# Attention and soft mixture of experts on one core: the attention loop written by pairs of heads, both heads' products with v in one run of 64-column tiles and one bank, and transposed x copied out of its bank by VectorE

## The chip, the core and the metric

The kernel runs on one core of one Trainium2 chip. Its engines work side by side, each through its own list of instructions in order: TensorE (PE, whose weight loads the profile shows apart as PEld), VectorE (DVE), ScalarE (ACT), GpSimd (POOL) and SyncE (SP), which here issues nearly all transfers from and to the main memory. An engine that waits for another holds everything that stands behind the waiting instruction in its list. The metric is device time in microseconds of one execution; a kernel is run several times and the median counts.

## The reference

Eight batches of twelve heads attend causally over 448 positions with 64 columns a head; the result is laid out as a matrix x of 3584 rows by 768 columns. A soft mixture of eight experts with four slots each follows.

```
scores = 0.125 * q @ k.T, -1e9 above the diagonal
attn = softmax(scores);  x = attn @ v               # per head; heads side by side in x
logits = x @ phi                                    # 3584 x 32
d = softmax of logits over the 3584 rows;  slot_input = d.T @ x
slot_out[e] = relu(slot_input[e] @ w1[e]) @ w2[e]   # 768 -> 1024 -> 768, four slots an expert
out = softmax of logits over the 32 slots @ slot_out
```

All is float32. The weights w1 and w2 are 50 MB together, q, k and v about 33 MB.

## The kernel before, in words

**Two stages.** The first goes through the 96 heads, as 48 pairs that share 128 partitions, and fills x, the logits and the slot inputs. The second goes through the experts and then through the rows of the output. Weight tiles of 768 KB (128 x 1536, `load_w`) are fetched in both: 23 (numbers 0 to 22) during the first stage, one with every other pair; numbers 23 to 34 into memory that the first stage gives back at its end (pool `wt1`), and the rest into tiles that are used again. SP issues its transfers in order, so a weight tile whose memory is still in use holds back those after it.

**One head.** The scores lie transposed, keys on partitions, in one tile of two banks (`s`; three such tiles, six of the eight banks). `scores1` adds the causal mask (a product of `tri` with a bf16 identity) and the product of k with q; `max_keys` (DVE, three instructions: one that transposes and reduces, two short ones) takes the maxima; `max_row` brings them into a row by a transpose on PE into `rt` and a reduction on DVE into `mr`; `max_spread` (POOL) writes them into rows of `r2`; `scores2` adds to the scores the product of `k2` with `r2`, which holds the row maxima and the rounding rest of q; `exps` (ACT) writes the exponentials to `pt`; `attv` multiplies them with v, with a column of ones for the sum, in tiles of 128 rows by 64 columns of the array; `norm` (DVE) divides by the sum and writes x. Around it, for each pair, ACT rounds k and q (`cast_k`, `cast_q`) and copies k (`copy_k2`), and POOL computes the rests (`sub_k`, `sub_q`). Each raw k or q (448 KB) has one of three buffers and is fetched anew as soon as its rest is computed.

**Where the order comes from.** Every engine runs in the order in which the program is written. Table `ORDER` gives it for a head: head i has its `scores2` and `exps`, head i+1 its `max_row`, head i+2 its `scores1`, and head i-1 its products with v and its `norm`, so PE alternates between scores and products of different heads.

**Two small banks.** Of the eight banks, one (`po`) takes the products with v of one head, four blocks of 65 columns, and one (`misc`, tag "m") is shared by everything small, one user at a time: `rt`, the transposed x of a pair (`xt`, copied to memory by ACT as `xts`), the logits of a batch in three parts (`g`, from two pairs each, `next_logits`), the slot input (`sp`, twice a batch, `dispatch`) and two transposes once a batch (`tp`, `logits_e`). In the table the steps with `g`, `xt`, `sp` and `tp` stand between `scores2` and `attv`.

**The last block of queries** has 64 rows, not 128. Its four products take the first 64 columns of the array and leave the other 64 empty; the products of the other three blocks come in twos, one for each half of the array.

Of the kernel before, what the change touches and what calls it, by code (L numbers as in the profile page):

```python
# [17 lines left out]
P = 128  # L18
# [14 lines left out]
NR, XB, XT = 2, 3, 3  # L33
# [14 lines left out]
ORDER = (  # L48
# [4 lines left out]
)  # L53

SC0, SC1, SC2, SC3 = 576, 0, 320, 512
RW, RC, RF = 96, 4, 20
CQ0 = (0, 128, 256, 384)
# [29 lines left out]
def attention_soft_moe(ctx: ExitStack, tc: tile.TileContext, qk, va, phi, w1, w2, out):  # L87
# [17 lines left out]
    qd_, kf_ = [fix.tile([P, 2, S], F32R, name="qd0")], [fix.tile([P, 2 * S + KP], F32R, name="ks0")]  # L105
    x_[1] = fix.tile([P, NCH, 3 * P], F32, name="x1")
    qd_.append(fix.tile([P, 2, S], F32R, name="qd1"))
    zero = fix.tile([P, P // 2], F32, name="zero")
    r_ = [fix.tile([P, RW], F32, name=f"r{i}") for i in range(2)]
    kf_.append(fix.tile([P, 2 * S + KP], F32R, name="ks1"))  # L110
# [3 lines left out]
    kf_.append(fix.tile([P, 2 * S + KP], F32R, name="k2"))  # L114
    *ks_, k2_ = (k[:, 0:2 * S].rearrange("p (h s)->p h s", h=2) for k in kf_)
# [88 lines left out]
    nc.vector.memset(zero, 0.0)  # L204
    nc.vector.tensor_copy(out=identb, in_=ident)
    for i in range(NR):
        nc.gpsimd.memset(r2_[i][0:64, :, :].bitcast(F32), 0.0)
        if i == 0:
            nc.vector.memset(k2_[0:64, :, :].bitcast(F32), 1.0)
    nc.vector.memset(pob, 0.0)  # L210
    for k in kf_:
        nc.vector.memset(k[:, 2 * S:2 * S + KP].bitcast(F32), 0.0)
    for i in range(2):
        nc.vector.memset(r_[i], -3.0e38)
# [12 lines left out]

    def cast_q(p, hs=slice(0, 2)):
        if p < NPAIR:
            nc.scalar.activation(out=qd_[p % NR][:, hs], in_=st["raw", 0, p][:, hs], func=AF.Copy)  # L230

    def cast_k(p, hs=slice(0, 2)):
        if p < NPAIR:
            nc.scalar.activation(out=ks_[p % NR][:, hs], in_=st["raw", 1, p][:, hs], func=AF.Copy)

    def sub_k(p, hs=slice(0, 2), eng=None):
        if p < NPAIR:
            ks = ks_[p % NR][64:P, hs]
            (eng or nc.gpsimd).tensor_tensor(out=ks, in0=st["raw", 1, p][64:P, hs], in1=ks, op=ALU.subtract)

    def copy_k2(p, hs=slice(0, 2)):
        if p < NPAIR:
            nc.scalar.activation(out=k2_[64:P, hs], in_=ks_[p % NR][0:64, hs],
# [8 lines left out]
    def scores1(i, part):  # L252
# [3 lines left out]
        ks, qd = kf_[p % NR], qd_[p % NR]  # L256
# [69 lines left out]
    def scores2(i, cs):  # L326
# [4 lines left out]
        k2, r2 = kf_[NR], r2_[p % NR]  # L331
# [9 lines left out]
    def attv(i, qcs):  # L341
        if not 0 <= i < NHD:
            return
        p, h = divmod(i, 2)
        pt, v, po = pt_[i % 2], va_[p % 2], st.get(("po", i), po0)
        begun = st.setdefault(("begun", i, id(po)), set())
        for qc in qcs:
            for c in range(qc + 1):
                col = SCOL[c] + P * (qc - c)
                for u in range(0, P if qc < 3 or i == NHD - 1 and c == 3 else 64, AW):  # L350
                    nc.tensor.matmul(po[u:u + AW, qc], pt[:, col + u:col + u + AW], v[:, c, h],
                                     start=u not in begun, stop=c == qc, skip_group_check=True)
                    begun.add(u)

    def norm(i, k):
        if not 0 <= i < NHD:
            return
        p, h = divmod(i, 2)
        if k == 0:
            if i % 6 == 0:  # L360
                xn = x_[p // 3 % XB]
                st["xn", p // 3] = xn
                for k in range(3):
                    st["x", p + k] = xn[:, :, P * k:P * k + P]
            sm = st["sm", i] = moe.tile([P, NCH], F32, tag="sm", name=f"sm{i}", bufs=2)
            nc.vector.tensor_scalar(out=sm, in0=st.get(("po", i), po0)[:, :, HD], scalar1=EPS, scalar2=None, op0=ALU.add)
        elif k == 1:
            nc.vector.reciprocal(out=st["sm", i], in_=st["sm", i])
        else:
            sm = st.pop(("sm", i))  # L370
            nc.vector.tensor_tensor(out=st["x", p][:, :, HD * h:HD * h + HD], in0=st.get(("po", i), po0)[:, :, 0:HD],
                                    in1=sm.unsqueeze(2).to_broadcast([P, NCH, HD]), op=ALU.mult)

    def xtrans(p):
# [5 lines left out]
        nc.scalar.activation(out=xt, in_=pt, func=AF.Copy)  # L383
# [64 lines left out]
    plan, plan_a = {}, {}  # L448
    for b in range(NB):
        o, last = 12 * b, b == NB - 1  # L450
        for j in range(PPB if not last else PPB - 2):
            plan_a[o + 2 * j + 4] = lambda p=b * PPB + j: xtrans(p)
        for j, r in ((0, 9), (2, 11)):
            plan[o + r] = lambda b=b, j=j: next_logits(b, j, misc(f"g{b}_{j}"))
        if not last:
            plan[o + 15] = lambda b=b: (next_logits(b, 4, misc(f"g{b}_4")), logits_b(b, lt))
            plan_a[o + 17] = lambda b=b: logits_e(b)
# [440 lines left out]
```

## Time and profile before

| | |
|---|---|
| median of 3 runs | 432.06 us (430.77 to 432.63) |
| profiled execution | 430.89 us |
| its span, first to last instruction | 429.2 us |
| busy: PE, PEld | 396.0, 317.6 us |
| busy: DVE, ACT, POOL | 297.6, 287.5, 266.2 us |
| mean clock granted to PE | 0.979 of full |
| read from and written to memory | 107.25 and 11.01 MB |

The span falls in two. Up to about 331 us the heads run, at about 240 GB/s of transfers; from there to the end the experts and the output run, at about 410 GB/s. A line of the profile names the engine, the operation and out<-in by the program's names; numbers of buffers are left out, so `r` stands for `r_` and for `r2_`, `ks` for both buffers of k. All instructions are recorded under line 71, that of the helper that keeps the order, so tiles tell them apart. An instruction's duration and the next one's start overlap by some 0.07 us on DVE, so steps are read from start to start.

### The profile page before, as it was taken

What the parts mean: (1) busy time and instruction counts of PE and PEld (TensorE: products, weight loads), DVE (VectorE), ACT (ScalarE), POOL (GpSimd) and SP (SyncE); (2) the same over time, 40 slices, a digit from 0 to 9 for tenths busy, and PEclk for the clock granted to TensorE, in tenths of its full rate; (3) what the DMA queues carried; (4) which work ended last, traced back from release to release, by engine and by line L of the source; (5) the groups of instructions that cost most, each with busy time, mean ns of one, the idle gap of its engine ahead of it and who ended that gap; (6) DMA issues with size and microseconds to landing.
All of it is one profiled execution on the core that took longest, in us unless ns stands there. A gap on an engine that the chain in (4) does not pass through costs nothing. (4 is left out here: it accounts for less than half of the span.)

```text
span 429.2 us, 14091 instructions
## 1 busy us (share of the span) xinstructions
PE 396.0 (92%) x5782; PEld 317.6 (74%) x5782; DVE 297.6 (69%) x861; ACT 287.5 (67%) x400; POOL 266.2 (62%) x216
## 2 busy tenths in 40 slices
PE   6898999999999999999999999999989998998740
PEld 3687888898898889888988888898868654544430
DVE  4687788778777877787787877778775477423440
ACT  5587879787887888887878788878865211333330
POOL 5799998888888788887887888888861000000000
PEclk8999999999999999999999999999999999999985
DMA  7476777777677776777776776677759999999997
GB/s 266 137 246 225 216 267 258 248 250 224 222 260 256 238 237 213 246 254 243 237 229 226 256 269 236 211 227 268 268 210 344 411 413 422 425 419 411 400 393 328
DMA packets 34481, 119.18 MB, mean 278 GB/s; under 512 B 3824, under 2 KB 8944, under 8 KB 32880
## 3 DMA queue, kind: packets, MB, share of 16 engines
q1 hardware_dynamic: 34272, 118.01, 77.5%
q8 instruction: 46, 0.75, 0.7%
q10 hardware_dynamic: 144, 0.27, 0.2%
q14 instruction: 19, 0.16, 0.1%
HBM read 107.25 MB, written 11.01 MB: 276 GB/s over the span
## 5 line engine op out<-in xcount | busy, mean ns | idle before, releaser
L71 ACT ACTIVATE pt<-s 128x1024 f32<-128x1024 f32 x96 | 98.2, 1023 | 57.2 <-PE s L71 51.8
L71 PEld LDWEIGHTS po<-va,pt 128*64 128x64 f32 x3040 | 117.8, 137 | 22.1 <-issue 21.6
L71 PE MATMUL po<-va,pt 128*64 128x65 f32 x3040 | 131.0, 225 | 0.0
L71 DVE TRANSPOSE_TENSOR_REDUCE r<-s 128x32 f32<-128x1024 f32 x96 | 118.2, 1231 | 2.4 <-PE s L71 2.0
L71 POOL TENSOR_TENSOR r<-qk,qd 64x896 fp32r<-64x896 f32 (+1 forms) x50 | 101.2, 2023 | 6.5 <-ACT qd L71 2.7
L71 POOL TENSOR_TENSOR ks<-qk,ks 64x896 fp32r<-64x896 f32 (+1 forms) x47 | 97.8, 2080 | 6.6 <-ACT ks L71 3.5
L71 POOL TENSOR_SCALAR_AFFINE_SELECT r<-mr 14x448 fp32r<-14x448 f32 x96 | 61.9, 645 | 47.5 <-DVE mr L71 43.4
L71 PE MATMUL s<-qd,ks 128*128 128x448 f32 (+3 forms) x384 | 76.5, 310 | 2.3 <-DVE ks L71 2.3
L71 PE MATMUL s<-r,k 128*128 128x320 f32 (+3 forms) x384 | 65.0, 290 | 3.5 <-ACT k L71 2.1
L71 PEld LDWEIGHTS s<-r,k 128*128 128x128 f32 (+1 forms) x384 | 54.3, 176 | 8.3 <-POOL r L71 5.6
L71 PEld LDWEIGHTS s<-qd,ks 128*128 128x128 f32 (+1 forms) x384 | 55.3, 182 | 3.1 <-DVE ks L71 2.5
L71 DVE TENSOR_SCALAR sm<-po 128x4 f32<-128x4 f32 x95 | 15.4, 162 | 52.9 <-PE po L71 51.8
L71 ACT ACTIVATE ks<-qk 128x896 fp32r<-128x896 f32 (+1 forms) x50 | 46.1, 923 | 8.1 <-DMA qk<-in_qk_dram 4.3
L71 ACT ACTIVATE qd<-qk 128x896 fp32r<-128x896 f32 (+1 forms) x50 | 46.1, 923 | 1.8 <-DMA qk<-in_qk_dram 1.7
L71 ACT ACTIVATE k<-ks 64x896 fp32r<-64x896 f32 (+1 forms) x49 | 45.8, 934 | 1.1
L71 DVE TENSOR_TENSOR x<-po,sm 128x256 f32<-128x256 f32 x95 | 40.3, 425 | 3.3
L71 PE MATMUL s<-tri,identb 128*128 128x64 bf16 (+2 forms) x288 | 39.6, 234 | 0.0
L71 PEld LDWEIGHTS <-identb 128*128 128x128 bf16 x339 | 35.0, 107 | 4.9 <-issue 3.1
L71 DVE TENSOR_REDUCE r<-r 128x16 f32<-128x32 f32 x192 | 34.1, 177 | 5.4
L71 PE MATMUL rt<-ident,r 128*76 128x128 f32 x96 | 28.8, 300 | 2.7 <-DVE sm L71 0.8
L71 PE MATMUL xt<-ident,x 128*128 128x128 f32 x188 | 29.7, 281 | 0.1
L71 DVE TENSOR_REDUCE mr<-rt 14x32 f32<-14x128 f32 x96 | 25.8, 269 | 3.8 <-PE rt L71 3.6
(136 smaller groups left out, 360.6 us busy)
## 6 DMA issues: line engine op xcount, KB each, us to landing
qk<-in_qk_dram SPq DMA_DIRECT2D x94, 448.0 KB, 4.0
w<-in_w_dram SPq DMA_DIRECT2D x43, 768.0 KB, 6.9
w<-in_w_dram SPq DMA_DIRECT2D x10, 1536.0 KB, 19.1
va<-in_va_dram SPq DMA_DIRECT2D x47, 260.0 KB, 3.2
out_dram<-ot SPq DMA_DIRECT2D x16, 384.0 KB, 6.7
out_dram<-ot SPq DMA_DIRECT2D x2, 1536.0 KB, 9.3
qk<-in_qk_dram SPq DMA_DIRECT2D x4, 224.0 KB, 3.4
hw<-in_w_dram SPq DMA_DIRECT2D x1, 768.0 KB, 6.4
```

What stands on the lines that cost most here:

```text
L71: return self._tc.keep_in_program_order(op(*args, **kwargs))
```

## The change

- The loop goes by pairs. `block(p)` writes for both heads a = 2p and a+1, in this order on PE: `scores2(a)`, `scores1(a+2)`, `scores2(a+1)`, [`tp`], `xt` of the pair before, `scores1(a+3)`, `attv(a)`, `rt(a+2)`, `attv(a+1)`, the last blocks of both heads (`attv3`), `rt(a+3)`, then `sp` or `g` where the pair has one.
- Both heads' products have one bank: seven blocks of 65 columns. The last blocks of the two heads are one block, head a in the upper 64 partitions and head a+1 in the lower; `attv3` alternates between them, so each fills one half of the array. `rt` takes 64 columns rather than 76, the same shape of tile as the products.
- `norm` is done once a pair: one sum, one reciprocal, one product for the full blocks of both heads and one for each last block.
- The copy of `xt` to memory goes from ACT to DVE, behind `max_keys(a+2)` and ahead of `max_keys(a+3)`.
- `sub_q(p+1)` stands in block p, no longer in pair p-1; the fetch of the raw k of pair p+3, which takes the buffer that it frees, follows it in the block, and so does that raw k's `cast_k(p+3)`, as the last of ACT's work. The fetch of v and of a weight tile stands at the block's start.
- `sp` of the seventh batch's second half is issued in the last block, behind `attv(a)`; before it was issued in the pair 45.
- Before the loop, `scores1` of head 2 and two runs of filling products go away and the work on the maxima of head 1 comes in. Two tiles rather than three hold `xts`; the rows 64 to 127 of the last block in x are zeroed once.

On PE, around the logits of pairs 14 and 15 (`rt34` to `rt37` are the rows of maxima of heads 34 to 37). Before:

```order
L71 MATMUL po_130<-va0_94,pt1_99 64x65 x16
L71 MATMUL rt36_2100<-ident_120,r0_90 76x128 [waits DVE_49,Activation_49]
...
L71 MATMUL s35_1994<-r21_96,k2_95 66x64
L71 MATMUL g2_2_2121<-xts14_1958,phi0_226 32x128 [waits DVE_49]
...
L71 MATMUL po_130<-va1_98,pt0_97 64x65 [waits DMAHW4_49]
L71 MATMUL po_130<-va1_98,pt0_97 64x65 x15
L71 MATMUL rt37_2154<-ident_120,r1_91 76x128 [waits DVE_49,PE_49]
```

Now:

```order
L65 MATMUL rt34_1982<-ident_119,r0_89 64x128 [waits DVE_49]
L65 MATMUL po_129<-va0_93,pt1_98 64x65 [waits Activation_49]
L65 MATMUL po_129<-va0_93,pt1_98 64x65 x11
...
L65 MATMUL rt35_2011<-ident_119,r1_90 64x128 [waits DVE_49,PE_49]
L65 MATMUL g16_2020<-xts14_1846,phi0_223 32x128 [waits DVE_49]
L65 MATMUL g16_2020<-xts14_1846,phi0_223 32x128 x3
L65 MATMUL g16_2020<-xts15_1949,phi1_224 32x128 x4
L65 MATMUL s34_1929<-r21_95,k2_94 128x448 [waits Activation_49,Pool_49]
```

Before, a whole head's products (16 instructions of the program) stood between the `g` and the next `rt`, and `scores2` ahead of `g`. Now `g` follows `rt35` at once, and `scores2` of head 34 follows `g`.

On DVE, in the block of pair 16 (heads 32 and 33). Now:

```order
L65 TENSOR_REDUCE r0_89<-s34_1929 128x2x16 [waits PE_49]
L65 TENSOR_REDUCE r0_89<-r0_89 128x2x8 [waits DVE_49]
L65 TENSOR_REDUCE r0_89<-r0_89 128x6 [waits DVE_49]
L65 COPY xts15_1949<-xt15_1944 128x512 [waits PE_49]
L65 TENSOR_REDUCE r1_90<-s35_1952 128x2x16 [waits PE_49]
L65 TENSOR_REDUCE mr34_1996<-rt34_1982 14x32 [waits PE_49,Pool_49]
L65 TENSOR_REDUCE r1_90<-r1_90 128x2x8 [waits DVE_49]
L65 TENSOR_REDUCE r1_90<-r1_90 128x6 [waits DVE_49]
L65 TENSOR_SCALAR sm16_2009<-po_129 128x7 [waits PE_49]
L65 TENSOR_REDUCE mr35_2013<-rt35_2011 14x32 [waits PE_49,Pool_49]
```

Before, `rt34` and `rt35` were reduced a head apart, each ahead of the maxima of the next head's scores; now the maxima of both heads, with the copy of `xt` between them, stand in a row ahead of `mr35`.

On SP, the weight tiles of `wt1` from number 25 on. Before:

```order
L71 DMA w_5532<-in_w_dram 128x1536 [waits Activation_49]
L71 DMA w_5534<-in_w_dram 128x1536 [waits DMAHW6_49,DVE_49,PE_49]
L71 DMA w_5536<-in_w_dram 128x1536 [waits PE_49,Activation_49]
```

Now:

```order
L65 DMA w_5417<-in_w_dram 128x1536 [waits DMAHW7_49,DMAHW6_49,Pool_49]
L65 DMA w_5419<-in_w_dram 128x1536 [waits DMAHW5_49,PE_49]
L65 DMA w_5421<-in_w_dram 128x1536 [waits DVE_49,PE_49]
L65 DMA w_5423<-in_w_dram 128x1536 [waits DVE_49]
```

The second row of the first piece and the third of the second are weight tile 26. By the addresses in both programs it takes the place of one buffer of k and of the end of `x1`, and PE's part of its wait is for the `sp` of the seventh batch's second half, which reads `x1` last. Tile 24 (first row now) waits for `sub_q` of the last pair in both.

```diff
-NR, XB, XT = 2, 3, 3
+NR, XB, XT = 2, 3, 2
...
-    pob = ps_1.tile([P, NCH * VC], F32, name="po")
-    po0 = pob.rearrange("p (a b)->p a b", b=VC)
+    pob = ps_1.tile([P, NQ * VC], F32, name="po")
+    po2 = pob.rearrange("p (a b)->p a b", b=VC)
+    po0 = po2[:, 0:NCH]
...
-            nc.tensor.transpose(out=st["rt", i][0:RW - RF, 0:P], in_=r_[i % 2][:, RF:RW], identity=ident)
+            nc.tensor.transpose(out=st["rt", i][0:AW, 0:P], in_=r_[i % 2][:, RF:RF + AW], identity=ident)
...
+    def attv3(p):
+        for c in range(NCH):
+            for h in range(2):
+                col = SCOL[c] + P * (NCH - 1 - c)
+                nc.tensor.matmul(po2[AW * h:AW * h + AW, NQ - 1], pt_[h][:, col:col + AW], va_[p % 2][:, c, h],
+                                 start=False, stop=c == NCH - 1, skip_group_check=True)
...
         xt = st["xt", p] = xtp.tile([P, 512], F32, tag="xt", name=f"xts{p}", bufs=XT)
-        nc.scalar.activation(out=xt, in_=pt, func=AF.Copy)
+        nc.vector.tensor_copy(out=xt, in_=pt)
...
+    def block(p):
+        a, b = 2 * p, p // 6 - 1
+        last, m6 = p == NPAIR - 1, p % 6
...
+        if p % 2 and p // 2 < RES:
+            load_w(p // 2)
+        scores2(a, range(NCH))
+        exps(a)
+        scores1_all(a + 2)
+        for k in range(3):
+            max_keys(a + 2, k)
+        scores2(a + 1, range(NCH))
+        if m6 == 2 and b >= 0 and p > 6:
+            logits_e(b)
+        if p:
+            xtrans(p - 1)
+        exps(a + 1)
+        scores1_all(a + 3)
+        max_keys(a + 3, 0)
+        sub_q(p + 1)
+        load_qk(p + 3, 1)
+        sub_k(p + 2)
+        load_qk(p + 3, 0)
+        if m6 == 1 and p > 6:
+            logits_d(b, lt)
+        copy_k2(p + 1)
+        cast_q(p + 2)
+        cast_k(p + 3)
+        if last:
+            attv(a, [(qc, qc, FULL if qc < 3 else FULL[0:1]) for qc in range(NCH)], po0, begun)
+            dispatch(NB - 2, 1)
...
+            return
+        attv(a, [(qc, qc, FULL) for qc in range(3)], po2, begun)
+        max_row(a + 2, 0)
+        attv(a + 1, [(qc, 3 + qc, FULL) for qc in range(3)], po2, begun)
+        max_row(a + 2, 1)
+        max_spread(a + 2)
+        for k in (1, 2):
+            max_keys(a + 3, k)
+        attv3(p)
+        norm(p, 0)
+        max_row(a + 3, 0)
+        max_row(a + 3, 1)
+        max_spread(a + 3)
...
+        if m6 in (3, 5) and p > 6:
+            sp = misc(f"sp{b}_{m6 // 5}")
+            dispatch_a(b, m6 // 5, sp)
+        for k in (1, 2):
+            norm(p, k)
...
+        if m6 in (2, 4) and p >= 2:
+            next_logits(p // 6, m6 - 2, misc(f"g{p}"))
+        elif m6 == 0 and p:
+            next_logits(b, 4, misc(f"g{p}"))
+            logits_b(b, lt)
```

More of the change, by code (lines that the diff above doesn't have):

```diff
@@ L349, in attv @@
                 col = SCOL[c] + P * (qc - c)
[L350 to L358, printed above, removed]
-        if k == 0:
[L360 to L366, printed above, removed]
+                for u, w in us:
+                    if u and qc == NCH - 1 and c < qc:
+                        continue
+                    nc.tensor.matmul(po[w:w + AW, k], pt[:, col + u:col + u + AW], v[:, c, h],
+                                     start=w not in begun, stop=c == qc, skip_group_check=True)
+                    begun.add(w)
@@ L495, in attention_soft_moe @@
         max_keys(1, k)
-    sub_q(1, h0)
+    max_row(1, 0)
+    max_row(1, 1)
+    sub_k(1, h1, nc.vector)
+    max_spread(1)
+    cast_k(2)
     sid = const.tile([P, NSLOT], F32, name="sid")
@@ L584, in attention_soft_moe @@
+    for p in range(NPAIR):
+        block(p)
+        if p == NPAIR - 1:
             scs.close()
```

173 lines of the change are left out of this document (66 added, 107 removed), and 4 rows, old and new, of the table ORDER.

## The prediction, made before the changed kernel was run

> **What bounds the kernel now.** I read first the busy time by stretches, then the waits, then ACT's exponentials as a clock of the heads, then single steps in the timeline. All sums below are made against the profiled execution (430.89 us, span 429.2); the median of the runs is 432.06, 1.17 above it, and the prediction is the median plus the sum. A measurement of this kernel can tell about 0.5% (2.2 us) from no change.
>
> ```profile
> core 0: us, PE busy (x) PEld busy (x) DVE busy (x) ACT busy (x) POOL busy (x), PEclk, DMA share, GB/s
> 80.00:120.00 40.00, 39.60 (x622) 34.58 (x621) 31.72 (x93) 32.97 (x43) 32.88 (x24) 1.00 0.72 240
> 355.00:360.00 5.00, 4.38 (x76) 2.08 (x72) 3.66 (x15) 0.86 (x3) 0.00 (x0) 1.00 1.01 426
> ...
> ACT pt L71 <- PE s L71: 51.8, 81, 3.7
> DVE sm L71 <- PE po L71: 51.8, 82, 2.1
> POOL r L71 <- DVE mr L71: 43.4, 78, 2.8
> PEld po L71 <- issue: 21.6, 89, 0.6
> ...
> L71 ACT ACTIVATE pt<-s x75: 1001/1024/1027, 70.6 to 316.0; 128x1024 f32<-128x1024 f32 x75
> L71 ACT ACTIVATE pt<-s x92: 1001/1025/1027, 27.5 to 330.2; 128x1024 f32<-128x1024 f32 x92
> ```
>
> In the heads PE is busy 99% of the time, and ACT and DVE wait for it: PE bounds this stage. 74 steps from 70.6 to 316.0 are 3.316 us a head, 6.63 a pair. In the experts (355 to 360) the transfers are full and bound the end.
>
> **What the change takes from PE.** One head's products with v:
>
> ```profile
> 123.71 0.64 PE L71 MATMUL g<-xts,phi 128*32 128x128 f32 x16
> 124.28 1.38 PE L71 MATMUL po<-va,pt 128*64 128x65 f32 x32
> 125.59 0.30 PE L71 MATMUL rt<-ident,r 128*76 128x128 f32 x1
> ```
>
> A product is recorded as two instructions. 24 of the 32 go in twos, 8 (the last block) alone: 20 steps in 125.59 - 124.28 = 1.31 us, 65 ns each. With both last blocks side by side a pair has 32 steps, not 40: 0.52 us less. One run in place of two saves one entry, 21.6/89 = 0.24 us by the wait above. So PE's work falls by about 0.76 of 6.63 us, to some 5.9 a pair. If nothing else ended later, that would be the new pair.
>
> **What takes its place.** In the new block PE issues `rt(a+3)`, then `g` or `sp`, then the next pair's `scores2`. `rt(a+3)` needs the maxima of head a+3, which stand on DVE behind those of a+2 and the new copy; `g` and `sp` need the one small bank, which DVE frees by reducing `rt`. The rows for each step:
>
> ```profile
> 126.41 0.68 PE L71 MATMUL s<-r,k 128*128 128x448 f32 x4
> 126.92 0.63 PE L71 MATMUL xt<-ident,x 128*128 128x128 f32 x4
> ...
> 20.32 0.25 PE L71 MATMUL s<-tri,identb 128*128 128x64 bf16 x2
> 21.21 1.25 DVE L71 TRANSPOSE_TENSOR_REDUCE r<-s 128x32 f32<-128x1024 f32 x1 [0.22 <-PE s L71]
> 22.50 0.40 DVE L71 TENSOR_REDUCE r<-r 128x16 f32<-128x32 f32 x2
> 23.04 0.28 PE L71 MATMUL rt<-ident,r 128*76 128x128 f32 x1
> ...
> 120.15 1.23 DVE L71 TRANSPOSE_TENSOR_REDUCE r<-s 128x32 f32<-128x1024 f32 x1
> 121.41 0.40 DVE L71 TENSOR_REDUCE r<-r 128x16 f32<-128x32 f32 x2
> 123.16 0.27 DVE L71 TENSOR_REDUCE mr<-rt 14x32 f32<-14x128 f32 x1
> 123.36 1.23 DVE L71 TRANSPOSE_TENSOR_REDUCE r<-s 128x32 f32<-128x1024 f32 x1
> 124.52 0.24 DVE L71 TENSOR_TENSOR lt<-g,mk 128x128 f32<-128x128 f32 x1
> ...
> L71 DVE COPY ot<-pp 128x384 f32<-128x384 f32 x26 | 13.6, 554 | 12.3 <-PE pp L71 12.2
> L71 DVE COPY c<-so 128x192 f32<-128x192 f32 x2 | 0.6, 352 | 2.1 <-PE so L71 2.1
> ...
> 14.67 0.28 PE L71 MATMUL rt<-ident,r 128*76 128x128 f32 x1
> 14.99 0.28 DVE L71 TENSOR_REDUCE mr<-rt 14x32 f32<-14x128 f32 x1 [1.96 <-PE rt L71]
> ...
> 327.13 0.28 DVE L71 TENSOR_REDUCE mr<-rt 14x32 f32<-14x128 f32 x1
> 327.46 0.42 PEld L71 LDWEIGHTS xt<-ident,x 128*128 128x128 f32 x4 [0.33 <-DVE mr L71]
> 327.48 0.64 POOL L71 TENSOR_SCALAR_AFFINE_SELECT r<-mr 14x448 fp32r<-14x448 f32 x1 [2.75 <-DVE mr L71]
> ...
> 317.58 0.85 PE L71 MATMUL sp<-x,gs 128*32 128x384 f32 x8 [0.80 <-DVE si L71]
> 318.36 1.24 PEld L71 LDWEIGHTS po<-va,pt 128*64 128x64 f32 x32 [0.63 <-issue]
> ```
>
> From the start of `scores2(a)`, at 0: `scores2` 0.51; `scores1(a+2)` until DVE can begin, 0.89 (20.32 to 21.21): 1.40. Large reduction 1.26 (120.15 to 121.41): 2.66. Two short ones, 0.40 with 0.07 overlap: 2.99. The copy of 512 columns is not in the trace as a DVE operation; 384 take 554 ns and 192 take 352, so 512 take 0.69, 0.62 with the overlap: 3.61. (From below it would be the 0.55 of 384 columns, from above that plus 192 more, 0.76; the slope is near both.) The second large reduction 1.16 (123.36 to 124.52): 4.77. `mr(a+2)` 0.20: 4.97. Two short ones 0.40: 5.37. `rt(a+3)` 0.14 later (22.90 to 23.04): 5.51. `mr(a+3)` 0.32 later: 5.83. Bank free 0.33 later: 6.16.
>
> PE by itself would be ready for `rt(a+3)` earlier: 0.51 + 0.69 + 0.51 + 0.47 (`xt`) + 0.69 + 32 steps of 65 ns + 0.12 = 5.07. So 0.44 us of the saving is waited out before `rt`, and about 0.5 more after it, until the bank is free. With `g` (0.57, 123.71 to 124.28) the block takes **6.73**; with `sp` (0.78, 317.58 to 318.36) **6.94**; with neither it ends by `scores2(a+2)`, whose rows come from `mr(a+2)` by POOL, 0.35 + 0.64 + 0.05 after 4.77: **5.81**. Where `tp` is emptied by ACT ahead of `xt` (pairs 8, 14, ... 44), up to one exponential, 1.02 us, comes on top, at least 0; I take 0.5, since ACT's copies are short and only their place behind the exponential is late: **7.23**.
>
> Of the 45 pairs 2 to 46, 9 have neither, 16 have `g`, 7 `g` with `tp`, 13 `sp`: 52.3 + 107.7 + 50.6 + 90.2 = 300.8 us. Before, from the exponential of head 4 (27.5) to that of head 94 (327.41, below) 299.9. **+0.9 us**: the loop hardly changes. The step with most weight is the bank wait; 0.1 us a pair is 4.5 us.
>
> What else moves is covered. The `norm` of a pair runs on DVE after `mr(a+3)` and is over before the next block's first large reduction at 1.40; uncovered it would cost about 1 us a pair. ACT loses the copy of `xt`, and it was waiting anyway. POOL keeps its work:
>
> ```profile
> L71 POOL TENSOR_TENSOR ks<-qk,ks 64x896 fp32r<-64x896 f32 x46 | 96.6, 2100 | 6.0 <-ACT ks L71 3.0
> L71 ACT ACTIVATE ks<-qk 128x896 fp32r<-128x896 f32 x46 | 43.9, 954 | 5.0 <-DMA qk<-in_qk_dram 1.2 <-ACT k L71 0.4
> DMA to landing us min/median/max: 3.0/4.1/5.8
> 15.34 1.09 POOL L71 TENSOR_SCALAR_AFFINE_SELECT r<-mr 14x448 fp32r<-14x448 f32 x1 [0.61 <-DVE mr L71]
> ```
>
> Two of 2.10 and two of 0.64 are 5.5 us of POOL in a block of 5.8 to 7.2.
>
> **Start.** The second `max_spread` ended at 16.43 in the trace; without `scores1` of head 2 (0.69) ahead of it on PE, it ends near 15.6. From there 2 x 2.10 + 0.64 on POOL to `scores2(2)` at 20.5, one plain block to 26.3, and 0.7 to the exponential of head 4: 27.0, 0.5 earlier, or 1.6 earlier if the rest is as tight; I take **-1.0**.
>
> **The end.** The transfers bound the rest, so what counts is how many weight tiles are in when SP runs free.
>
> ```profile
> 314.00:330.76 16.76, 15.71 (x246) 12.57 (x244) 10.46 (x32) 8.76 (x11) 5.98 (x7) 1.00 0.89 317
> 327.41 1.02 ACT L71 ACTIVATE pt<-s 128x1024 f32<-128x1024 f32 x1 [0.96 <-ACT k L71]
> ```
>
> 330.76 is 3.35 us after the exponential of head 94. Until then 16.76 x 317 GB/s = 5.3 MB came, two loads of v among them: about 6 tiles of 0.79 MB. In the changed kernel tile 26 waits for the last `sp`, behind the last block's `attv`: exponential from 0.70 to 1.72, products 1.31, `sp` 0.78, signals 0.2, so 4.05, 3.35 after that exponential. Only tiles 22 to 25 are in by then; 27 to 30 queue behind 26. Two tiles at 426 GB/s are **+3.8 us**. If the gap is closed by slack in the experts it is 0, and with the last block's 1.2 us shorter work, -1.2; the full transfers at 355 speak for the upper end.
>
> **Sum.** +0.9 - 1.0 + 3.8 = +3.7: 434.6 for the profiled execution, **436 us** for the median.
>
> **Rivals.**
> 1. *PE stays the bound.* For it: 99% busy, all others waiting. PE's work a pair is 5.07 + 0.23 for `rt` and the way out, `g` 0.57 in half the pairs, `sp` 0.78 in 13 of 45: 5.82; 45 x 0.81 = 36 less, 432 - 36 + 2.8 = **399 us**. Against it: the program makes PE wait for DVE at `rt(a+3)` and for the bank at `g`. Chance 0.06. (The Trainium skill, Perfetto Trace Analysis, "Identifying the Most-Contended Engine", says to optimize the engine with the highest occupancy first; by that rule the saving would come through whole. The trace agrees on which engine that is, and shows waits of DVE for PE that the new order turns round.)
> 2. *The chain is shorter than summed*, by 0.3 us a pair: DVE's maxima or the bank come sooner than rows from other places say. 13.5 less: **423 us**. For it: 11 links, each bounded by its nearest row. Chance 0.19.
> 3. *The raw k is late* (slower still). It is fetched only when `sub_q` is over, 2.3 us into the block, and its cast stands before the next pair's first exponential. That exponential must be over at 2.1 + 0.6 (the slack of DVE there) for nothing to be late: cast from 7.4 at the latest, so the fetch may take 5.1 us. Landing is 4.1 in the median, 5.8 at most, and every other pair a weight tile is on the way. At 0.5 us late in 23 pairs: 436 + 12 = **448 us**. Chance 0.14.
> 4. *PE's clock falls*, since it now idles 0.4 to 0.9 us a pair. The row of 355 to 360 has PE idle 12% of the time in such pieces, and a granted clock of 1.00; half the clock would add PE's 5.82 us a pair, near 700 us in all. Chance 0.02. (The Trainium skill, TensorE: Matmul & The Clock Gate, "A second HAM failure mode: psum-queue depth-cycling", reports micro-idles between groups that bring the slow clock back; the trace's own row does not bear it out.)
> 5. *The last blocks don't run side by side.* Then PE's work is 0.52 longer, 0.44 of it inside the wait before `rt`: 0.08 a pair, 4 us, inside the forecast's range; no chance of its own.
>
> **Chances and range.** Forecast 0.55, own range 430 to 442; 0.04 for none of these, near no change. Faster: 0.06 + 0.17 of rival 2 + 0.02 = 0.25. Slower: 0.40 of the forecast + 0.16 = 0.56. Same: 0.19. The range takes in rivals 2 and 3: 422 to 449.
>
> **What would show it.** Right: PE busy near 86% in the loop, waiting for DVE before the second `rt` and again before `g` and `sp`; pairs of 5.8, 6.7, 6.9 and 7.2 us in the order of a batch; weight tile 26 issued about 3.4 us after the exponential of head 94. The run of products near 2.1 us a pair shows the saving, whatever the time. Wrong: pairs of equal length near 5.9 (rival 1); ACT waiting for raw k ahead of exponentials (rival 3); a granted clock under 1 in the loop (rival 4); tile 26 issued before the loop's end.

## The result, and the profile after

The changed kernel takes 458.44 us in the median of four runs (458.20 to 459.87), the kernel before in the same comparison 431.41 (430.72 to 432.63): a ratio of 1.063, with a 95% interval of 1.059 to 1.067. It is slower, by seven times what was forecast (27.0 us between the medians, 3.9 forecast). The profiled execution took 459.87 us, 28.98 more than that of before. Of the kernels below, one run of e3_hold, at 451.80 us, was in a slow state of the chip and is left out of its median.

Where that lies is read from ACT's exponentials. This is the row of the changed kernel that groups those of heads 4 to 94 (count; shortest, median and longest in ns; first and last start):

```profile
L65 ACT ACTIVATE pt<-s x91: 1002/1026/1034, 28.4 to 352.3; 128x1024 f32<-128x1024 f32 x91
```

Against 27.5 and 327.41 before, the first comes 0.8 us later, the last 24.0 us later than that, and the end of the span (458.2) stands 105.9 us behind the last, not 101.8: **start +0.8, loop +24.0, end +4.1**. Forecast were -1.0, +0.9 and +3.8.

Busy time by stretches, first of the kernel before, then of the changed one (stretch and its length, PE, PEld, DVE, ACT and POOL busy, clock granted to PE, share and GB/s of the transfers):

```profile
120.00:320.00 200.00, 197.17 (x3097) 171.41 (x3096) 157.56 (x456) 162.89 (x210) 164.39 (x120) 1.00 0.72 240
50.00:60.00 10.00, 9.85 (x158) 8.73 (x156) 8.21 (x26) 7.79 (x9) 9.49 (x9) 1.00 0.85 298
```

```profile
50.00:60.00 10.00, 8.77 (x92) 7.26 (x92) 4.50 (x11) 4.78 (x5) 5.41 (x5) 0.66 0.45 163
120.00:320.00 200.00, 183.22 (x2923) 150.16 (x2921) 164.03 (x426) 141.94 (x166) 153.96 (x113) 1.00 0.71 224
```

PE was busy 99% of the middle of the loop and is busy 92% of it now; no other engine has taken its place. And near the start there is a stretch with PE's clock at 0.66, in which 92 instructions of PE are recorded where the kernel before has 158. The waits of the changed kernel (engine and tile, what it waited for; us in all, times, longest):

```profile
ACT pt L65 <- PE s L65: 49.0, 64, 3.2
ACT ks L65 <- DMA qk<-in_qk_dram: 48.3, 37, 3.0
PE g L65 <- DVE mr L65: 10.2, 23, 0.4
PE xt L65 <- ACT lg L65: 7.8, 7, 2.0
PE sp L65 <- DVE mr L65: 5.8, 13, 0.4
DVE x L65 <- PE sp L65: 5.7, 7, 0.9
PE s L65 <- POOL r L65: 5.7, 5, 2.2
```

PE now waits for DVE ahead of every `g` and `sp`, as forecast; it also waits for ACT ahead of seven `xt`, for POOL five times, ACT waits for raw k, and the products of `norm` (`x`, on DVE) wait for seven of the `sp`.

One pair that ends with a `g` (pair 12), in the timeline of the changed kernel (start and length in us; in brackets the idle time before it and what ended it):

```profile
103.59 0.74 PE L65 MATMUL s<-r,k 128*128 128x448 f32 x4
...
107.76 1.39 PE L65 MATMUL po<-va,pt 128*64 128x65 f32 x40
108.64 0.37 DVE L65 TENSOR_REDUCE r<-r 128x16 f32<-128x32 f32 x2
109.16 0.27 PE L65 MATMUL rt<-ident,r 128*64 128x128 f32 x1
109.54 0.28 DVE L65 TENSOR_REDUCE mr<-rt 14x32 f32<-14x128 f32 x1 [0.18 <-PE rt L65]
109.88 0.65 PE L65 MATMUL g<-xts,phi 128*32 128x128 f32 x16 [0.45 <-DVE mr L65]
110.45 0.74 PE L65 MATMUL s<-r,k 128*128 128x448 f32 x4
```

The pair takes 6.86 us (103.59 to 110.45; 6.73 were forecast). DVE's last short maxima end at 109.01 and PE's products at 109.15: both arrive at the second `rt` together. From the `rt` to `g` 0.72 us pass, in which DVE reduces `rt` and frees the bank.

With a pair counted from its `scores2(a)` to the next one's, the starts in the timeline give, for pairs 9 to 46 by their number modulo 6 (medians; the forecast beside them):

| pair mod 6 | 0 (`g`) | 1 (neither) | 2 (`tp`, `g`) | 3 (`sp`) | 4 (`g`) | 5 (`sp`) |
|---|---|---|---|---|---|---|
| forecast | 6.73 | 5.81 | 7.23 | 6.94 | 6.73 | 6.94 |
| changed kernel | 6.86 | 5.90 | 8.4 (8.1 to 9.2) | 7.07 | 7.05 | 7.07 |

Pairs 4, 5 and 6 stand apart: 10.23, 10.05 and 8.46 us.

### The profile page after: what moved, and what is told of

Read it like the earlier page. It is cut to its first block, busy times and chain, and to the rows that moved or that the text cites. A ratio compares the mean times of both kernels' runs of the same rounds, so it can differ in the third digit from the quotient of the medians.

```text
span 458.2 us, 14013 instructions
## 1 busy us (share of the span) xinstructions
PE 394.4 (86%) x5763; PEld 299.4 (65%) x5763; DVE 325.4 (71%) x864; ACT 267.3 (58%) x353; POOL 264.3 (58%) x215
## 4 chain that ended last, share of the span: by engine, by line
PE 45%; DMA 18%; DVE 7%; issue 6%; POOL 5%; ACT 3%; DVEq 0%; POOLq 0%; ACTq 0%; SPq 0%
PE s L65 17%; PE po L65 14%; DMA w<-in_w_dram 13%; DMA qk<-in_qk_dram 5%; POOL r L65 4%; PE xt L65 4%; DVE r L65 3%; PE rt L65 3%; PE sp L65 3%; DVE mr L65 2%; PE g L65 2%; ACT pt L65 1%; PE pp L65 1%; PE hp L65 1%; PE e L65 1%
## 5 line engine op out<-in xcount | busy, mean ns | idle before, releaser
L65 PE MATMUL po<-va,pt 128*64 128x65 f32 x3040 | 110.2, 225 | 0.1
L65 PEld LDWEIGHTS po<-va,pt 128*64 128x64 f32 x3040 | 97.0, 138 | 18.0 <-issue 11.9
L65 PE MATMUL s<-qd,ks 128*66 128x64 f32 (+3 forms) x384 | 80.5, 321 | 2.2 <-DVE ks L65 2.0
L65 ACT ACTIVATE ks<-qk 128x896 fp32r<-128x896 f32 (+1 forms) x50 | 45.9, 920 | 54.9 <-DMA qk<-in_qk_dram 48.3
L65 PEld LDWEIGHTS s<-r,k 128*128 128x128 f32 (+1 forms) x384 | 59.7, 176 | 24.4 <-POOL r L65 17.8
L65 PE MATMUL s<-r,k 128*128 128x448 f32 (+3 forms) x384 | 66.4, 296 | 6.2 <-POOL r L65 5.7
L65 PE MATMUL s<-tri,identb 128*128 128x128 bf16 (+2 forms) x288 | 43.5, 239 | 1.3 <-ACT pt L65 1.3
L65 DVE COPY xts<-xt 128x512 f32<-128x512 f32 x47 | 32.1, 683 | 8.4 <-PE xt L65 8.4
L65 PEld LDWEIGHTS <-identb 128*128 128x128 bf16 x320 | 28.0, 102 | 6.2 <-issue 5.0
L65 DVE TENSOR_TENSOR x<-po,sm 128x384 f32<-128x384 f32 (+2 forms) x49 | 26.7, 547 | 7.2 <-PE sp L65 5.7
L65 PE MATMUL rt<-ident,r 128*64 128x128 f32 x96 | 27.6, 288 | 0.9
```

The source lines that it names most:

```text
L65: return self._tc.keep_in_program_order(op(*args, **kwargs))
```

## Experiments

All but the first are built on the first, so that a disturbance near the loop's start doesn't blur them. "Loop" is from the exponential of head 4 to that of head 94, "end" from there to the end of the span, both from the kernel's own trace; the time is the median of its runs. The trace is that of one execution: the changed kernel's and e5_actcopy's were the slowest of their runs (459.87 and 453.80 us). The start isn't compared: e7_all and e11_tp_sp, which do the same work up to head 4, reached it at 27.8 and 26.8 us.

| kernel | time, us | loop | end |
|---|---|---|---|
| before (all comparisons) | 430.9 to 431.5 | 299.9 | 101.8 |
| changed | 458.44 | 323.9 | 105.9 |
| e1_setup | 451.24 | 315.3 | 106.3 |
| e2_cast | 446.23 | 311.1 | 106.2 |
| e3_hold | 445.38 | 311.3 | 106.9 |
| e4_apart | 458.69 | 323.5 | 106.5 |
| e5_actcopy | 448.96 | 316.7 | 106.2 |
| e6_wlate | 446.49 | 311.1 | 106.3 |
| e7_all | 437.93 | 302.4 | 106.8 |
| e8_tail | 448.01 | 317.2 | 102.2 |
| e9_early_sp | 441.51 | 312.6 | 100.5 |
| e10_early_tp | 442.13 | 311.8 | 100.3 |
| e11_tp_sp | 429.15 | 300.3 | 100.3 |
| e12_spread | 426.55 | 296.1 | 101.4 |

### The stall in pairs 4 to 6

The timeline of the changed kernel around the end of pair 4, rows of POOL and what it serves:

```profile
45.46 0.26 DVE L65 TENSOR_REDUCE mr<-rt 14x32 f32<-14x128 f32 x1
46.08 0.21 POOL L65 TENSOR_SCALAR_AFFINE_SELECT sid<-sid 128x32 f32<-128x32 f32 x1
46.51 0.77 POOL L65 TENSOR_SCALAR_AFFINE_SELECT sid<-sid 128x32 f32<-128x32 f32 x3 [0.22 <-POOL sid L65]
...
47.36 2.08 POOL L65 TENSOR_TENSOR r<-qk,qd 64x896 fp32r<-64x896 f32 x1
...
49.51 0.64 POOL L65 TENSOR_SCALAR_AFFINE_SELECT r<-mr 14x448 fp32r<-14x448 f32 x1
50.21 0.81 PE L65 MATMUL s<-r,k 128*128 128x448 f32 x4 [2.25 <-POOL r L65]
```

`mr` of head 10 was there at 45.7, but its `max_spread` came at 49.51: ahead of it in POOL's list stand the four selects that prepare `sid`, and a `sub_q` of 2.08 us. The list of POOL's instructions in the changed kernel shows that this is its order, not a wait (`r_95` belongs to pairs 5 and 7, `r_92` to pair 6):

```
TENSOR_TENSOR r_95<-qk_5_465,qd_88 64x896
TENSOR_TENSOR ks_86<-qk_6_572,ks_86 64x896
AFFINE_SELECT sid<-sid 128x32 x4
TENSOR_TENSOR r_92<-qk_6_575,qd_85 64x896
AFFINE_SELECT r_95<-mr_705 14x448
TENSOR_TENSOR ks_91<-qk_7_671,ks_91 64x896
AFFINE_SELECT r_95<-mr_722 14x448
```

The program writes these selects two at a time, behind the spreads of two blocks. In the list all four stand together and ahead of those spreads, and the `sub_q` and `sub_k` of the next block have come ahead of them as well: here the list does not have the order of the program, as the description above had it. **e1_setup** moves the preparing work:

```diff
+    for f in later:
+        f()
     max_row(0, 1)
     max_spread(0)
...
-        for _ in range(2):
-            if later and p:
-                later.pop(0)()
```

> All of POOL's preparing work (mk, run_m, run_z, si, sid with its four selects, srep) goes ahead of the first max_spread, where POOL was idle; the rest is the changed kernel. Theory S (the four selects of sid in POOL's list put sub_q of later pairs ahead of the spreads of pairs 5 to 7, PE stood still and its clock fell): pairs 4, 5 and 6 go from 10.2, 10.1 and 8.5 us to the 7.05, 5.90 and 6.86 of later pairs of their kind, so about 9 us less, 449 us, and a granted clock of 1.00 from 50 to 60 us. Rival (ACT's wait of 2.4 to 2.7 us for raw k in the same pairs is the cause): at most 1 us less, 457 us, and the clock still falls.

Measured: 451.24 us. Its trace has 315.3 us for the loop, 8.6 less (the medians differ by 7.2), and its row for the same stretch reads

```profile
50.00:60.00 10.00, 9.25 (x175) 7.64 (x173) 8.70 (x24) 7.15 (x8) 7.82 (x8) 1.00 0.68 206
L65 ACT ACTIVATE pt<-s x91: 1002/1027/1037, 27.1 to 342.4; 128x1024 f32<-128x1024 f32 x91
```

with the clock at 1.00. Theory S stands. Pair 5 takes 5.88; pairs 4 and 6 keep 7.98 and 7.21, for the reason of the next experiments.

### Raw k and the pairs with tp

The chain of waits of the changed kernel, at the start of pair 26 (`tp`, 9.20 us):

```profile
197.55 5.41 DMA qk<-in_qk_dram
...
203.06 0.04 ACT ks L65
...
203.92 0.18 ACT pt L65
...
204.82 0.27 ACT gs L65
205.09 0.18 ACT lg L65
...
205.31 0.65 PE xt L65 x4
```

Raw k lands 5.41 us after its fetch is issued; then follow, on ACT one behind the other, its cast, the first exponential, `tp`'s two copies, and only then `xt` gets the bank. Two kernels take raw k out of this chain in different places. **e2_cast** moves the cast:

```diff
         if p:
             xtrans(p - 1)
+        cast_k(p + 2)
         exps(a + 1)
...
         cast_q(p + 2)
-        cast_k(p + 3)
```

> As e1_setup, and cast_k of a pair stands one block later, between tp's copies and the second exponential, so that no first exponential stands behind a wait for raw k. Theory K1 (the late raw k costs only in the seven pairs with tp, where tp's copies stand behind the exponential and xt behind them): these go from 8.4 to about 7.5, the others stay: 6 us less than e1_setup. Rival K2 (every late exponential costs): 10 to 20 us less. Rival K3 (tp is late by its place behind the exponential, whatever raw k does): 0 to 1 us less.

**e6_wlate** leaves the cast and moves the transfer of the weight tile:

```diff
-        if p % 2 and p // 2 < RES:
-            load_w(p // 2)
...
         load_qk(p + 3, 0)
+        if p % 2 and p // 2 < RES:
+            load_w(p // 2)
```

> As e1_setup, but the weight tile of every other pair is fetched behind both raw transfers of the block and not at its start. Theory K1 (raw k is late because it shares the transfer engines with a weight tile, 4.6 to 4.8 us to landing instead of 3.4, and in the seven pairs with tp this is paid): raw k always lands 5.6 to 5.8 us into the block, no first exponential waits, tp pairs 8.24 to about 7.8 as in e2_cast: 3 to 5 us less than e1_setup. Rival (order on ACT alone, not the transfer): no change.

Measured: 446.23 and 446.49 us, 5.0 and 4.8 less than e1_setup, and in both the loop is 4.2 shorter. The pairs with `tp` go from 8.24 in the mean to 7.87 and 7.81, four irregular ones (4, 6, 36 and 40) to 6.9 to 7.2; all others stay within 0.04. Theory K1 stands, K2 falls, and K3 is not the cause of these 4.2 us, though it holds for what is left in the pairs with `tp`. How ACT's wait for raw k in e6_wlate is left at

```profile
ACT ks L65 <- DMA qk<-in_qk_dram: 44.5, 42, 2.7
PE xt L65 <- ACT lg L65: 3.8, 7, 0.5
```

while nothing is lost to it shows that its 48.3 us were no measure of the damage: most of that wait ends before the exponential can start anyway. What stays is 0.5 us of `xt` waiting for `tp`'s copies in each of the seven pairs, whatever raw k does.

### What stands at the second rt

**e4_apart** lets the two heads' last blocks run one after the other:

```diff
-        for c in range(NCH):
-            for h in range(2):
+        for h in range(2):
+            for c in range(NCH):
```

> As e1_setup, but the last blocks of the two heads come one after the other, not in turns, so that the eight products don't run side by side. Theory A (the prediction's: DVE's chain ends after PE at the second rt, PE has 0.44 us to spare): 0.08 us a pair, about 4 us more than e1_setup. Theory B (PE's own list lasts until the second rt): 0.45 to 0.52 us a pair, 21 to 24 us more.

Measured: 458.69 us, 7.5 more than e1_setup; pairs with `g` or `sp` are 0.19 to 0.24 longer, those with neither the same. Neither number was right. The run of products of both, first e1_setup, then e4_apart:

```profile
189.69 0.92 PE L65 MATMUL po<-va,pt 128*64 128x65 f32 x24
...
190.77 1.39 PE L65 MATMUL po<-va,pt 128*64 128x65 f32 x40
```

```profile
203.23 1.67 PE L65 MATMUL po<-va,pt 128*64 128x65 f32 x40
```

Running in turns saves 0.28 us a pair, not 0.52. Of it 0.2 are paid at the second `rt` when they are gone; so PE has less than 0.1 us to spare there, not 0.44.

**e5_actcopy** takes the copy away from DVE:

```diff
-        nc.vector.tensor_copy(out=xt, in_=pt)
+        nc.scalar.activation(out=xt, in_=pt, func=AF.Copy)
```

> As e1_setup, but ACT copies the transposed x again, behind the first exponential; DVE's list is 0.62 us a pair shorter. Theory A (the prediction's chain: DVE alone sets the second rt and PE has 0.44 us to spare there): some 0.4 us less in 36 pairs, 16 us less than e1_setup. Theory B2 (DVE's maxima and PE's own list reach the second rt together, within 0.1 us, in pair 28 at 5.62 and 5.71 of the block): at most 2 us less; and more time than e1_setup where the second exponential, which now stands behind the copy, is late for its products.

Measured: 448.96 us, with ranges that overlap (448.19 to 453.80 against 450.39 to 453.30 for e1_setup); in its trace, of the slowest run, the loop is 1.4 longer. Pairs with neither gain 0.24, those with `g` or `sp` 0.05 to 0.1, those with `tp` lose 0.4, and pair 8 alone, where the pause ahead of `xt` grew to 2.5 us, took 11.45. DVE is done well ahead of the second `rt` here (at 195.36, in a pair with neither):

```profile
194.99 0.37 DVE L65 TENSOR_REDUCE r<-r 128x16 f32<-128x32 f32 x2
195.92 0.30 PE L65 MATMUL rt<-ident,r 128*64 128x128 f32 x1
```

0.62 us less on DVE buy almost nothing: Theory A falls, B2 stands. DVE's maxima and PE's list arrive together, and behind them the wait for the bank is paid in full.

### The bank behind the second rt

**e3_hold** lets `g`, and the second `sp` of a batch, wait for the next block, where `scores2(a)` runs while DVE frees the bank:

```diff
         scores2(a, range(NCH))
+        for f in held:
+            f()
+        held.clear()
...
+        if m6 == 5 and p > 6:
+            held.append(lambda: dispatch(b, 1))
...
-            next_logits(p // 6, m6 - 2, misc(f"g{p}"))
+            held.append(lambda: next_logits(p // 6, m6 - 2, misc(f"g{p}")))
```

> As e1_setup, and g of every pair and the second sp of a batch stand one block later, behind the next scores2(a). Theory B (PE's own list lasts until the second rt, and the wait for the small bank behind it, 0.72 us from rt to g, comes on top of it): the wait is covered by scores2, 0.45 to 0.65 us less in some 28 pairs, 13 to 18 us less than e1_setup. Rival (the wait only moves to xt, which then waits for the same bank): 0 to 4 us less.

Measured: 445.38 us, 5.9 less, between the two. Where raw k isn't late the wait is covered (pairs 4, 5 and 0 modulo 6 took 7.06, 7.06 and 6.86 us, 20.98 together, and take 6.09, 6.56 and 6.76, 19.41). But shorter pairs leave raw k less time; in pair 32 its cast began 2.9 us into the block:

```profile
233.50 0.95 ACT L65 ACTIVATE ks<-qk 128x896 fp32r<-128x896 f32 x1 [3.40 <-DMA qk<-in_qk_dram]
234.36 1.01 ACT L65 ACTIVATE pt<-s 128x1024 f32<-128x1024 f32 x1
```

and that pair took 10.5 us. **e7_all** is e1_setup, e2_cast, e3_hold and e6_wlate in one.

> e1_setup, e2_cast, e3_hold and e6_wlate in one kernel. If the late raw k took back e3_hold's gain (there its cast began up to 2.9 us into a block), the gains add: pairs of 6.7, 6.7, 6.7, 7.7, 6.1 and 6.5 us, 6.7 in the mean against 7.03 of e1_setup, so 14 us less than e1_setup, about 437 us; PE's own list, 6.5 us a pair, is the lower bound, 427 us. If the waits only move (rival), no less than e2_cast or e3_hold alone, 446 us.

Measured: 437.93 us, 13.3 less than e1_setup; pairs of 6.76, 6.69, 6.80, 7.74, 6.09 and 6.55 us. The loop is 12.8 us shorter, more than the 4.2 and 4.0 of e2_cast and e3_hold together: e3_hold's gain was held back by raw k. PE is busy 97% of the loop's middle in e7_all:

```profile
120.00:320.00 200.00, 193.36 (x3042) 157.92 (x3040) 172.29 (x449) 147.49 (x179) 161.57 (x118) 1.00 0.73 238
```

### The end

In the changed kernel the fetch of weight tile 26 stands at 355.56, 3.3 us behind the exponential of head 94 (3.4 were forecast), and SP's longest wait for an `sp` is

```profile
SPq L65 <- PE sp L65: 8.2, 1, 8.2
```

**e8_tail** issues that `sp` at the end of pair 46:

```diff
     for p in range(NPAIR):
         block(p)
+        if p == NPAIR - 2:
+            dispatch(NB - 2, 1)
...
-            dispatch(NB - 2, 1)
```

> As e1_setup, but sp of the seventh batch's second half is issued at the end of pair 46, behind its g, and not in the last block. Theory W (weight tile 26 waits for this sp and holds back tiles 27 to 30): tile 26 is issued some 4 to 5 us before the 3.3 us behind the exponential of head 94 of e1_setup, and the end comes 2 to 3 us sooner against that exponential, less 1.3 us for the sp in pair 46. Rival (another tile of the row waits as long for the loop's end): the next tile holds instead, and nothing is gained.

Measured: 448.01 us. Tile 26 is issued 0.7 us ahead of that exponential, 4.0 earlier, and the end comes 4.0 us sooner against it, more than expected; pair 46 takes 8.77 instead of 7.05, and the time is 3.2 less than that of e1_setup. Theory W stands, and with it the cause of the forecast's 3.8.

### Towards a faster kernel

**e9_early_sp** is e7_all with the second `sp` of every batch one step earlier:

```diff
-        if m6 == 5 and p > 6:
+        if m6 == 3 and p > 6:
             held.append(lambda: dispatch(b, 1))
...
-            dispatch(NB - 2, 1)
```

> As e7_all, and the second sp of every batch stands at the start of the pair with m6 = 4, behind its scores2(a), so it is covered there and the last block has none. By PE's own list the sum of a batch's six pairs stays 40.6 us (the one with m6 = 4 goes from 6.1 to 6.8, the one with m6 = 0 from 6.8 to 5.9): the loop 302 us as in e7_all, and the end as in e8_tail, 102.5 us behind the exponential of head 94 instead of 106.8: 4 us less than e7_all, 434 us. If the gain of e8_tail came from the longer pair 46 alone (rival), no change.

Measured: 441.51 us, 3.6 more than e7_all. The end came as expected (100.5), but the pairs with 4 modulo 6 took 8.05, not 6.8 (one, in which PE's clock fell, 9.34). Both `sp` in the timeline:

```profile
204.23 0.85 PE L65 MATMUL sp<-x,gs 128*32 128x384 f32 x8 [0.44 <-DVE mr L65]
206.97 0.85 PE L65 MATMUL sp<-x,gs 128*32 128x384 f32 x8 [1.22 <-DVE si L65]
```

The second waits for the bank until DVE has added the first to `si`. That stands behind the products of `norm`, and these wait 0.85 us for the first `sp`: by the program they write the buffer of x that it reads. The expectation counted PE's list and left out who holds the bank.

**e10_early_tp** goes back to the cast of e6_wlate, and empties `tp` first:

```diff
         held.clear()
+        tp = m6 == 2 and p > 6
+        if tp:
+            logits_e(b)
         exps(a)
...
         exps(a + 1)
+        if tp:
+            logits_r(b)
```

(`logits_r` is the update of `run_z`, cut out of `logits_e`.)

> As e9_early_sp without the moved cast, and tp stands right behind scores2(a), its copies by ACT ahead of the first exponential. The wait of xt for tp's copies, 0.9 us in seven pairs, is then covered: these pairs go from 6.8 to 6.0 to 6.2 us, 4 to 5 us less than e9_early_sp, about 430 us. Rival: the first exponential, 0.6 us later, makes its products or the third score tile late by as much, and nothing is gained: 434 us.

Measured: 442.13 us, no different from e9_early_sp. The pairs with `tp` fell to 6.1 to 6.7, as expected; but their successors rose from 7.74 to as much as 8.46, since in the shorter pairs the cast of raw k stands ahead of exponentials again (PE waits for a late exponential seven times, 4.6 us in all; e11_tp_sp below, with the cast moved, has 7.73).

**e11_tp_sp** puts together what had held: e7_all, the early `tp`, and the early `sp` for the seventh batch alone.

```diff
+        if p == NPAIR - 3:
+            held.append(lambda: dispatch(b, 1))
         if m6 == 5 and p > 6:
             held.append(lambda: dispatch(b, 1))
```

> As e7_all, with tp and its copies right behind scores2(a) as in e10_early_tp, and the second sp moved to the start of pair 46 for the seventh batch alone, since in e9_early_sp it waited there 1.2 us for the small bank behind DVE's si in every batch. Pairs with tp 6.8 to about 6.3 us, pair 46 8.0 instead of 6.1: loop 302.4 - 7 x 0.5 + 2 = 301 us, the end 100.5 us behind the exponential of head 94: 430 to 431 us, no difference to the kernel before. If the cast between the exponentials makes the second exponential late in the pairs with tp (rival), 434 us.

**e12_spread** also gives every user of the small bank a `scores2(a)` of its own:

```diff
-NR, XB, XT = 2, 3, 2
+NR, XB, XT = 2, 3, 3
...
+        if m6 == 2 and p > 6:
+            held.append(lambda: dispatch(b, 0))
...
-        if m6 in (2, 4) and p >= 2:
-            held.append(lambda: next_logits(p // 6, m6 - 2, misc(f"g{p}")))
+        if m6 in (3, 4):
+            held.append(lambda: next_logits(p // 6, 2 * m6 - 6, misc(f"g{p}")))
```

> As e11_tp_sp, with three buffers of xts; the first sp of a batch stands at the start of the pair with m6 = 3 and the first g at the start of the one with m6 = 4, so that each step on the small bank stands behind a scores2(a) and none behind a second rt. By the bank theory no pair then pays the 0.45 us from the second rt to the bank: 6.8, 6.7, 6.3, 6.8, 6.55 and 6.55 us, 6.6 a pair; loop 299 us, 428 us, 0.7% under the kernel before. If PE waits for the bank elsewhere (rival), as e11_tp_sp.

Measured: 429.15 us for e11_tp_sp, a ratio to the kernel before of 0.996 (0.994 to 0.998), and 426.55 us for e12_spread, **0.989 (0.986 to 0.991)**. The pairs of e12_spread take 6.76, 6.69, 6.22, 6.76, 6.55 and 6.56 us (pair 46, with its early `sp`, 8.14), and PE is busy 98% again. Still left is a wait of the weight loads of `scores2` for POOL's spread (14.3 us in 49 waits; before, 5.6 in 10):

```profile
120.00:320.00 200.00, 196.54 (x3116) 160.30 (x3116) 175.16 (x459) 148.55 (x181) 163.42 (x120) 1.00 0.74 241
...
PEld s L65 <- POOL r L65: 14.3, 49, 1.2
...
L65 ACT ACTIVATE pt<-s x91: 1004/1026/1037, 27.0 to 323.1; 128x1024 f32<-128x1024 f32 x91
```

With PE busy 99 and 98% the kernel before takes 299.9 us for the loop and this one 296.1: 0.08 us a pair is the most that the loop has gained in any of these kernels.

## Why the prediction was right, and where it was wrong

**Right: the direction, the chain on DVE and the bank, and the end.** Slower, because PE gives its saving back at the second `rt` and at the bank: the waits are there, 36 of them ahead of `g` and `sp`, and pairs with neither, with `g` and with `sp` came within 0.09 to 0.32 us of 5.81, 6.73 and 6.94. DVE's copy took 0.68 us (0.69). Tile 26 was issued 3.3 us behind the exponential of head 94 (3.35), and the end cost 4.1 us (3.8; by the prediction's own figures two tiles of 0.79 MB at 426 GB/s are 3.7); e8_tail shows that the `sp` was the cause.

**Wrong: the size, 29 us where 3.7 were forecast.** The loop was to cost 0.9 and cost 24.0. The 23.1 between them, by the runs:

| what the sum had | what the runs showed | us |
|---|---|---|
| "POOL keeps its work": 5.5 us of load in a block, so no cost | its list had another order; PE stood still and its clock fell (e1_setup) | 8.6 |
| raw k late: left to rival 3 | paid in the pairs with `tp` and some early ones (e2_cast, e6_wlate) | 4.2 |
| `tp`: 0.5 us on top of a pair with `g`, "since ACT's copies are short" | without late raw k still 7.81 instead of 7.23, seven times | 4.1 |
| the blocks with `g`, `sp` or neither | 0.32 too short for `g` behind the first `sp` of a batch, 0.13 for `sp` and the other `g`, 0.09 for neither: 7 x 0.32 + 20 x 0.13 + 9 x 0.09 | 5.7 |

That is 22.6 of 23.1. Each row comes from one trace of each kernel, in which single pairs with `tp` differ by up to 1 us, and the traced run of the changed kernel is 1.4 us above its median, so the split is good to 1 or 2 us.

The step that failed first is the sentence on **POOL**. It compared POOL's load with the length of a block, and an engine with enough time can still be late: what counts is what stands ahead of the instruction that PE waits for. The list of POOL, which shows the four selects and the `sub_q` ahead of the spreads, was there to be read before any run; the prediction read those of PE, DVE and SP.

The second is **`tp`**, a term of the right kind with the wrong size. The prediction put "up to one exponential, 1.02 us", and took half. At 7.81 instead of the 6.86 of a pair with `g` alone, `tp` costs 0.95 us even without late raw k, nearly the whole exponential. The chain of pair 26 shows all of the exponential in front of the copies, and in front of that a cast that waits for raw k. Rival 3 had this link and its sign (ACT waiting for raw k ahead of exponentials) was seen; its price of 0.5 us in 23 pairs was not. It cost 4.2 us, 2.6 to 3.0 of them in the seven pairs with `tp`, in which ACT has a second thing to do for PE.

The third is the **0.2 us behind the first `sp` of a batch**. The prediction had `norm` over "before the next block's first large reduction". That holds in pair 12, behind a second `sp`: DVE has added `sp` to `si` 0.99 us into the block and begins the large reduction at 1.53. In pair 16, behind a first `sp`, the products of `norm` wait 0.85 us for that `sp`, `si` is done only at 1.80 and the large reduction begins at 1.73; `xt`, which needs the bank that `si` empties, comes at 1.96 instead of 1.79, and the second `rt` at 5.76 instead of 5.57. So the first kind takes 7.05 and the second 6.86. The prediction followed the bank as far as the end of the block and no further; e9_early_sp shows the same wait at 1.22 us.

**PE's side was wrong, and it didn't show.** PE was to be ready for the second `rt` at 5.07 us and to wait 0.44 for DVE; it was ready at 5.56 (109.15 less 103.59), with DVE. The sum left out the 0.23 of the first `rt`, and took the products at 2.08 us where their two runs take 0.85 and 1.4; side by side they save 0.28 a pair (e4_apart), not 0.52. Since DVE's chain was summed rightly to 5.51, the pair came out nearly right; that PE's list, half a microsecond longer than summed, ended with it and not behind it was luck. But the saving on PE, 0.76 us a pair in the prediction, was hardly there to be given back, and rival 1 (399 us) was out of reach: e12_spread, with most waits gone, gains 0.08 a pair. Where the rest went can be read from PE's starts over heads 28 to 88: against before, the products take 2.27 us a pair instead of 2.65 and `xt` 0.47 instead of 0.56, but the steps from the two `rt` to what follows them take 0.56 instead of 0.28, `scores1` 1.57 instead of 1.44 and `scores2` 1.12 instead of 1.09. Part of the `rt` steps is the wait for POOL's spread. The sign "PE busy near 86%" was therefore wrong too, it was 92%; "pairs of 5.8, 6.7, 6.9 and 7.2" was right but for the last.

**The clock** was given 0.02 as a rival, for idles of 0.4 to 0.9 us, and in the steady loop of the changed kernel it stayed at 1.00. It fell where POOL made PE stand still for 2.25 us, inside the 8.6 us of the first row; how much of them is the clock's part and how much the stall's was not measured apart. From the 6.8 us at 0.54 shown below, the clock's part is some 3 us (an estimate). The rival wasn't empty: in e9_early_sp the clock fell once in the steady loop, behind waits of 0.45 and 1.22 us.

**Open.** The start was forecast 1.0 us earlier and came 0.8 later; since two kernels with the same start differ by 1 us there, the cause of these 1.8 us can't be read from the runs. Why `scores1` takes longer in the new order, and why the first `rt` holds PE longer, was not measured either.

## What to carry to other kernels

Read the list of every engine that PE waits for, not its load: a few short preparing instructions in the wrong place of an in-order list cost 8.6 us here, more than anything else that the prediction had left out. Where one small bank has many users, follow it from each user to the next one over the block's edge, with the instruction that frees it and all that stands ahead of that; work on the bank is cheap where another product of PE covers its handover, as `scores2(a)` does in e12_spread. And before a saving on the bounding engine is counted, sum that engine's list in the new order, instruction by instruction, and see what its neighbours then wait for: here 0.76 us a pair were counted and 0.08 came out.

## What the runs showed of the hardware

PE's clock fell after short pauses, but the length of a pause alone didn't decide. In the changed kernel (48.0 to 50.2 is the pause; the column with 0.54 is the clock):

```profile
48.00:50.20 2.20, 0.00 (x0) 0.00 (x0) 0.72 (x3) 0.95 (x1) 2.08 (x2) 1.00 1.18 310
50.20:57.00 6.80, 6.11 (x34) 5.05 (x36) 2.68 (x5) 3.62 (x4) 2.74 (x2) 0.54 0.62 230
...
203.40:205.30 1.90, 0.00 (x0) 0.00 (x0) 0.91 (x3) 1.90 (x5) 1.90 (x2) 1.00 0.16 60
205.30:210.00 4.70, 4.24 (x85) 3.54 (x89) 3.09 (x9) 3.89 (x5) 1.96 (x3) 1.00 0.66 199
```

A pause of 2.25 us was followed by 6.8 us at about half the clock; one of 1.97 us (203.35 to 205.31) by none of that. In e3_hold, after a pause of 2.73 us:

```profile
235.70:240.00 4.30, 4.25 (x46) 3.56 (x48) 2.06 (x3) 3.94 (x5) 0.91 (x1) 0.60 0.57 185
```

In e4_apart a pause of 2.62 us (11.75 to 14.37) was followed by none:

```profile
11.80:14.30 2.50, 0.00 (x0) 0.00 (x0) 0.89 (x2) 0.77 (x1) 2.22 (x10) 1.00 0.89 245
14.40:21.20 6.80, 6.80 (x99) 6.04 (x100) 4.39 (x12) 5.29 (x6) 5.99 (x5) 1.00 0.36 115
```

And in e9_early_sp it fell for 3.4 us with no pause longer than 1.22 us, after a stretch in which PE was busy 1.82 us of 3.40:

```profile
160.40:163.80 3.40, 1.82 (x15) 0.85 (x13) 2.19 (x7) 1.04 (x2) 2.85 (x3) 1.00 0.92 296
163.90:167.30 3.40, 3.40 (x17) 2.08 (x18) 0.99 (x2) 0.72 (x1) 2.16 (x2) 0.50 0.79 274
```

What else decides, such as where in time a pause falls, these runs don't show.

The Trainium skill, TensorE: Matmul & The Clock Gate, "HAM oscillation — how this bites in real kernels", warns of pauses above some 3.4 us; here one of 2.25 us was enough, and in e9_early_sp two of 0.45 and 1.22 us.

Products in both halves of the array in turns are not twice as fast: the 16 recorded products of the last blocks took 0.47 us in turns (1.39 less the 0.92 of the 24 that were the same) and 0.75 one after the other, a factor of 1.6. The Trainium skill, TensorEngine Tiling (Array Packing), "Theoretical Speedup", gives up to 2 for such tiles.
